# First weight transfer of a windowed-attention and mixture-of-experts kernel cut in two, with the middle steps of its hand-written schedule in a new order

## The chip, the core and the metric

The kernel runs on one core of one Trainium2 chip. The metric is device time in microseconds (us): the median of several runs, each of them one execution of the whole program. Times inside the program come from one profiled execution and count from the first instruction.

## The reference

Eight sentences of 576 tokens go through causal sliding-window attention (8 heads of 64, a window of 64 tokens), and then each sentence as a whole through one of eight experts:

```python
scores = np.where(mask, scale * (q @ k.T), -1e9)     # mask: 0 <= pos_q - pos_k < 64
attn = exp(scores - max) / sum
x = attn @ v                                          # (8, 576, 512)
logits = x.mean(axis=1) @ w_gate                      # one expert for each sentence
e = argmax(logits); gate = softmax(logits)[e]
out[b] = gate * (np.maximum(x[b] @ w1[e], 0) @ w2[e]) # w1[e]: 512x1024, w2[e]: 1024x512
```

All inputs and the output are 32-bit floats in the chip's main memory (HBM). Nothing of a sentence's expert weights can be loaded before the sentence's attention is done, since the choice of the expert depends on it.

## The kernel before

**Units and chunks.** The attention of a sentence (a batch b) is five units: four pairs of heads over the first 512 tokens, and one tail unit with the last 64 tokens of all heads. Unit number u is 5b + i, with i = 4 for the tail. A unit passes through these steps, each named by a letter and the unit's number:

- T (L225, tail L232): TensorE turns q and k round against an identity matrix, into PSUM. U and k (L242, L246, L252, L255) copy the two halves to SBUF, on ScalarE (Ua, ka) or VectorE (Ud, kd).
- S (L275): scores, sixteen small matmuls. With b in the name (Sb) two matmuls ahead of them (L269) put the mask in as a bias; without it, step K (L297) multiplies the mask in afterwards, on VectorE.
- E (L288, L291): exponential on ScalarE. l (L309, L314): row sums on TensorE. n and R (L351, L357): logarithm and exponential on ScalarE, which make a reciprocal.
- A (L331, L339): probabilities times v, on TensorE. X (L364, L370): the scaled result on VectorE, with a running sum for the gate.

The letter m in a T, S or A step takes its PSUM tile from a pool of three tiles that the experts use too; the other T, S, A and l steps have one buffer of their own each.

When the five X of batch b are done, the gate follows: g (L380, L384, VectorE), j (L392, TensorE), G (L403 to L407, VectorE: the largest logit and its index), H (L432, ScalarE), I (L438, VectorE), and P (L413), in which GpSimd loads the expert's number into a register.

The expert's work on a sentence is 18 chunks, always taken in the same order by the step c: eight of eight matmuls against w1 (L461), one for the tail tokens (L470), eight halves of four output rows against w2 (L503), and one for the tail (L512). After a chunk, ra or rd moves its result out of PSUM on ScalarE or VectorE (L446, L448, L482, L487). O and o store results.

**Loads.** Nearly all loads are issued by GpSimd, in its program's order, and turn 32-bit floats into 16-bit ones on the way: Q2b and Q2b+1 (L110: q and k of batch b, 512 KB each as they land), L (L141, L145: v of batch b, numbers 5b to 5b+4, 128 KB each and 64 KB for the fifth), t (L133: the tail of q and k, twice 64 KB), W (L423, L426: the weights; batch b has 4b and 4b+1 for the halves of w1, 4b+2 and 4b+3 for the halves of w2, 512 KB each). GpSimd's DMAs take eight semaphores in turn, so an issue waits until the DMA issued eight before it has landed. Step V (L150, L151) copies v of a batch into a shifted layout on VectorE and needs that batch's first four L.

**Order.** Each engine runs its instructions in the order in which the string OPS names the steps. OPS has 890 steps, read one by one at the end of the kernel function. A chunk's first operand waits for its weights, and everything behind it on TensorE waits with it.

Of the kernel before, what the change touches and what calls it, by code (L numbers as in the profile page):

```python
# [1 line left out]
OPS = (  # L2
# [35 lines left out]
).split()  # L38

# [17 lines left out]
def kernel(  # L57
# [13 lines left out]
    F = moe_w1.shape[2]  # L71
# [51 lines left out]
    def cast_raw(x, lohi, e):  # L123
        lo, hi = int(lohi) // 10, int(lohi) % 10
        tiles, tag = ((qms, "qm"), (kms, "km"))[x]
        if 0 not in tiles:
            tiles[0] = ld.tile([128, H, 256], BF16, tag=tag, name=tag)
        copy(e)(out=tiles[0][:, lo:hi], in_=raw[x, lo])
# [29 lines left out]
    mb = const.tile([128, 4, 16], FP16)  # L158
# [76 lines left out]
    def copy(e):  # L235
        return nc.scalar.copy if e == 'a' else nc.vector.tensor_copy
# [176 lines left out]
        nc.gpsimd.load(ereg, eidxs[b][0:1, 0:1])  # L413
        esl[b] = nc.gpsimd.snap(ereg, donate=True)

    def load_w(x):
        b, c = divmod(x, 4)
        s = WSLOT[b]
        e = ds(esl[b], 1)
        kw = {}  # L420
        if c < 2:
            cols = ts(c, F // 2)
            nc.gpsimd.dma_start(out=w1b[s][:, :, cols], in_=w1e[e].squeeze(0)[:, :, cols], **kw)  # L423
        else:
            fbs = ts(c - 2, 4)
            nc.gpsimd.dma_start(out=w2b[s][:, fbs], in_=w2e[e].squeeze(0)[:, fbs], **kw)  # L426
# [63 lines left out]
    def store(eng):  # L490
        for n, (dst, src) in enumerate(outq.pop(0)):
            (nc.scalar if n and eng is nc.sync else eng).dma_start(out=dst, in_=src)  # L492
# [43 lines left out]
    with tc.manual_schedule():  # L536
        for op in OPS:
            c, x = op[0], op[1:].lstrip("abdm")
            e = op[1:len(op) - len(x)]
            if c == "c":  # L540
                todo.pop(0)()
            elif c in "oO":
                store(nc.sync if c == "o" else nc.gpsimd)
            elif c == "r":
                evac.pop(0)(e)
            elif c == "F":
                wps = ps_m.tile([128, 512], FP32, tag="mo", name="wps")
                for _ in range(int(x)):
                    nc.tensor.matmul(out=wps, lhsT=warm[:, 0:128], rhs=warm, start=True, stop=True)
            elif c in setup_ops:  # L550
                setup_ops[c]()
            elif c == "Y":
                load_raw(int(x.split(".")[0]), x.partition(".")[2])
            elif c == "C":
                cast_raw(int(x.split(".")[0]), x.partition(".")[2], e)
            elif c == "Q":
                load_qk(int(x.split(".")[0]), x.partition(".")[2])
            elif c in batch_ops:
                batch_ops[c](int(x))
            elif c in unit_eops:  # L560
                unit_eops[c](*units[int(x)], e)
            else:
                unit_ops[c](*units[int(x)])
# [30 lines left out]
```

## Time and profile before

| | before |
|---|---|
| median of 3 runs | 203.64 us (203.49 to 203.77) |
| profiled execution, first to last instruction | 201.9 us |
| profiled execution's own whole time | not told by its page |
| TensorE (matmul) busy | 183.5 us, 91% |
| ScalarE busy | 131.8 us, 65% |
| VectorE busy | 119.9 us, 59% |
| GpSimd busy (issuing DMAs) | 111.0 us, 55% |
| moved by DMA, as it lands | 41.16 MB, mean 204 GB/s |

The profiled span is 1.7 us shorter than the median, which includes what lies around the program's instructions. In the profile PE is TensorE, PEld its weight loads, DVE VectorE, ACT ScalarE, POOL GpSimd. A timeline row gives start and length in us, engine, line, operation, out<-in, shapes and a count, and in brackets the idle time before it with what ended that. A matmul's row ends with a modelled end, so the time that a group really takes is the distance to the next group's start. A DMA's row on POOL is its issue; when it landed is told by the list of DMA issues, as us from the issue's start.

### The profile page before, as it was taken

Reading aid. Unit: us, or ns where it says so; the run is one execution under the profiler, and the core shown is the slowest. Engines: PE = TensorE matmul, PEld = TensorE weight load, DVE = VectorE, ACT = ScalarE, POOL = GpSimd, SP = SyncE. Lnnn points to the kernel's source line nnn. Section 1 sums busy time; section 2 is a strip of 40 time slices with the busy share of each in tenths; the row PEclk is TensorE's granted clock in tenths of the full one; section 3 lists DMA queues with packets and bytes.
Section 4 is the critical chain, followed back from the end, with each engine's and each line's share of the span. In section 5 each row is a group of like instructions: output and inputs, shape, how many; then the busy total and the mean of one; then the engine's idle time right before and its main releaser. Section 6 shows DMA issues by size and latency. Waiting matters only on the chain.

```text
span 201.9 us, 8105 instructions
## 1 busy us (share of the span) xinstructions
PE 183.5 (91%) x3518; PEld 124.2 (62%) x3522; DVE 119.9 (59%) x347; ACT 131.8 (65%) x247; POOL 111.0 (55%) x158
## 2 busy tenths in 40 slices
PE   0487886899999999999999999999999999999991
PEld 0455564656677756577667666676656666776760
DVE  3527989595477546895877457966494651216410
ACT  2179998876599578977779975757787436321121
POOL 7985939235931593478633552439452716553561
PEclk9999999999999999999999999999999999999998
DMA  6999999999999999999999999999999999999693
GB/s 135 175 188 159 194 162 198 199 198 174 196 201 197 170 198 193 174 201 167 200 206 200 169 195 223 259 208 137 183 237 243 266 254 212 274 212 301 235 325 134
DMA packets 83346, 41.16 MB, mean 204 GB/s; under 512 B 48080, under 2 KB 80976, under 8 KB 83312
## 3 DMA queue, kind: packets, MB, share of 16 engines
q0 software_dynamic: 81936, 39.72, 138.5%
q1 hardware_dynamic: 768, 0.85, 1.3%
q8 instruction: 27, 0.44, 0.8%
q10 hardware_dynamic: 608, 0.08, 0.2%
q14 instruction: 7, 0.06, 0.1%
HBM read 61.88 MB, written 9.44 MB: 353 GB/s over the span
## 4 chain that ended last, share of the span: by engine, by line
PE 77%; DMA 9%; POOL 7%; issue 3%; DVE 2%; ACT 1%; POOLq 0%; DVEq 0%; ACTq 0%
PE ph L461 28%; PE po L503 25%; DMA vw<-in_v_dram 9%; PE tp L225 5%; PE ph L470 4%; PE s L275 4%; PE av L331 3%; PE po L512 3%; PE lb L309 3%; POOL vw L141 2%; POOL km L110 2%; POOL qm L110 1%; POOL out_dram L492 1%; PE gps L392 1%; POOL qkt L133 1%
## 5 line engine op out<-in xcount | busy, mean ns | idle before, releaser
L503 PE MATMUL po<-w2b,hm 128*64 128x512 f16 x512 | 60.1, 379 | 0.0
L461 PE MATMUL ph<-xm,w1b 128*64 128x512 f16 x512 | 60.0, 379 | 0.0
L461 PEld LDWEIGHTS <-w1b 128*64 128x64 f16 x512 | 31.7, 110 | 18.7 <-issue 0.4
L503 PEld LDWEIGHTS <-hm 128*64 128x64 f16 x512 | 30.1, 110 | 19.3
L141 POOL DMA_DIRECT2D vw<-in_v_dram x32 | 28.9, 910 | 13.3 <-DMA w1b<-in_moe_w_dram 4.3
L446 ACT ACTIVATE hm<-ph,gw 128x512 f16<-128x512 f32 x39 | 26.6, 693 | 13.4 <-PE ph L461 13.3
L492 POOL DMA_DIRECT2D out_dram<-ob x31 | 17.2, 557 | 25.0 <-DMA w1b<-in_moe_w_dram 7.0
L351 ACT ACTIVATE ln<-lb 128x512 f32<-128x512 f32 (+1 forms) x40 | 22.5, 563 | 11.8 <-PE lb L309 8.6
L364 DVE CUSTOM_DVE_ANT_0 xm<-av,rl 128x512 f16<-128x512 f32 x32 | 21.6, 686 | 10.4 <-PE av L331 9.5
L482 ACT COPY ob<-po 128x512 f32<-128x512 f32 x18 | 10.6, 586 | 23.6 <-PE po L503 23.6
L448 DVE TENSOR_SCALAR hm<-ph,gw 128x512 f16<-128x512 f32 x25 | 18.7, 748 | 12.1 <-PE ph L461 11.6
L357 ACT ACTIVATE rl<-ln 128x512 f32<-128x512 f32 (+1 forms) x40 | 23.3, 594 | 1.5 <-DVE pool L364 1.3
L225 PE MATMUL tp<-ident,qm 128*64 128x128 bf16 x256 | 13.8, 232 | 7.4 <-DMA qm<-in_q_dram 6.9
L288 ACT ACTIVATE pe<-s 128x1024 f16<-128x1024 f32 x19 | 19.5, 1028 | 1.4 <-PE s L275 0.7
L297 DVE TENSOR_TENSOR pe<-pe,mask 128x1024 f16<-128x1024 f16 x24 | 16.3, 687 | 3.9 <-ACT pe L288 3.1
L252 ACT COPY kT<-tp 128x512 bf16<-128x512 bf16 x19 | 11.2, 597 | 9.0 <-PE tp L225 8.0
L225 PEld LDWEIGHTS <-qm 128*64 128x64 bf16 x256 | 10.7, 118 | 10.0 <-DMA qm<-in_q_dram 6.9
L482 DVE COPY ob<-po 128x512 f32<-128x512 f32 x14 | 9.7, 690 | 10.7 <-PE po L503 10.5
L423 POOL DMA_DIRECT2D w1b<-in_moe_w_dram x16 | 12.6, 785 | 5.9 <-DMA vw<-in_v_dram 2.9
L275 PEld LDWEIGHTS <-kT 64*128 64x128 bf16 x576 | 10.1, 95 | 8.9 <-issue 5.6
L331 PEld LDWEIGHTS <-vw 128*64 128x64 f16 x512 | 12.4, 112 | 4.7 <-issue 1.2
L225 PE MATMUL tp<-ident,km 128*64 128x128 bf16 x256 | 13.9, 231 | 1.4 <-DMA km<-in_k_dram 0.9
(80 smaller groups left out, 267.2 us busy)
## 6 DMA issues: line engine op xcount, KB each, us to landing
w1b<-in_moe_w_dram POOLq DMA_DIRECT2D x16, 512.0 KB, 9.3
w2b<-in_moe_w_dram POOLq DMA_DIRECT2D x16, 512.0 KB, 13.4
out_dram<-ob POOLq DMA_DIRECT2D x31, 256.0 KB, 8.1
vw<-in_v_dram POOLq DMA_DIRECT2D x32, 128.0 KB, 9.0
km<-in_k_dram POOLq DMA_DIRECT2D x7, 512.0 KB, 9.3
qm<-in_q_dram POOLq DMA_DIRECT2D x7, 512.0 KB, 9.0
out_dram<-obt POOLq DMA_DIRECT2D x14, 64.0 KB, 7.7
qkt<-in_q_dram POOLq DMA_DIRECT2D x8, 64.0 KB, 7.6
```

The costliest lines, as they stand in the source:

```text
L141: nc.gpsimd.dma_start(out=vt[:, 2 * J + 1], in_=v[b, :, 128 * J:128 * J + 128].rearrange("h c d -> c h d"))
L225: nc.tensor.transpose(tp[p0:p0 + 64, n, r], t[:, 2 * i + hh, ts(r, 64)], ident)
L288: nc.scalar.activation(out=po, in_=sp[0], func=AF.Exp, scale=scale)
L351: nc.scalar.activation(out=ln, in_=lb[:, 0:n], func=AF.Ln)
L357: nc.scalar.activation(out=rl, in_=lns.pop((b, i)), func=AF.Exp, scale=-1.0)
L364: nc.vector.tensor_tensor_reduce(out=xm[:, i], in0=av.rearrange("q r p -> q (r p)"), in1=rl, scale=1.0, scalar=0.0, op0=ALU.mult, op1=ALU.add,
L446: nc.scalar.activation(out=o, in_=i, func=AF.Relu, scale=g)
L448: nc.vector.tensor_scalar(out=o, in0=i, scalar1=g, scalar2=0.0, op0=ALU.mult, op1=ALU.max)
L461: nc.tensor.matmul(out=ph[64 * c:64 * c + 64], lhsT=w1t[:, kb, ts(2 * ft + c, 64)], rhs=xm[:, kb], start=(kb == 0), stop=(kb == 3), skip_g ...
L482: copy(e)(out=ob, in_=po)
L492: (nc.scalar if n and eng is nc.sync else eng).dma_start(out=dst, in_=src)
L503: nc.tensor.matmul(out=po[64 * c:64 * c + 64], lhsT=hm[:, fb, ts(2 * r + c, 64)], rhs=w2t[:, fb], start=(fb == 0), stop=(fb == 7), skip_gr ...
```

## The change

Two things change. The step W0 (the first half of the first batch's w1) becomes two transfers, W0.0 and W0.1, of a quarter of w1 each: 256 of the 1024 columns, enough for two w1 chunks each. And the steps from the 75th to about the 560th stand in a new order. Among them some copies change between ScalarE and VectorE, ten ra become rd, and some S change between b and no b (four Sb before, three after, one of these for a tail unit). The steps before and behind keep their order, so that the whole list has 892 steps.

```diff
-    "n2 R1 R4 l0 V0 A3 Ud6 L7 Am1 n0 E5 T9 X3 Am2 Ud9 S7 R2 L8 E7 Ud8 X1 R0 l5 X2 L6 n5 Smb6 "
...
-    "A9 W2 E10 S13 kd18 Ud18 L13 Tm15 Ud15 l10 Am8 R8 W3 kd15 ka17 T16 K14 L11 c X8 L14 n10 "
...
+    "E12 n8 K12 W0.1 Am7 E14 R6 A6 l12 Sm10 S11 n12 E10 T17 X7 l9 X6 A9 c ka17 n9 W1 Ud17 c R9 "
+    "K10 l10 E11 X9 rd R8 c rd S13 A8 X8 E13 rd T16 c rd W2 L11 g1 c c rd W3 Ua16 n10 ra j1 "
...
-    def load_w(x):
+    def load_w(x, part=""):
...
-            cols = ts(c, F // 2)
+            cols = ts(2 * c + int(part), F // 4) if part else ts(c, F // 2)
...
+            elif c == "W":
+                load_w(int(x.split(".")[0]), x.partition(".")[2])
```

OPS is one line shorter, so line numbers behind it are one lower than before up to load_w. Three places follow at which the order differs; a row has line, operation, out<-in with the buffers' numbers, and the written shape.

GpSimd up to the first weights, before (qkt is the tail of q and k, qm and km are q and k of batch 3, w1b0 the first batch's w1, vw2 v of batch 2, TENSOR_LOAD the step P0):

```order
L141 DMA vw1_92<-in_v_dram 128x8x64 x4
L133 DMA qkt_647<-in_q_dram 64x8x64
L133 DMA qkt_647<-in_k_dram 64x8x64
L110 DMA qm_703<-in_q_dram 128x8x256
L110 DMA km_820<-in_k_dram 128x8x256
L413 TENSOR_LOAD eidx_733
L423 ISA
L423 DMA w1b0_96<-in_moe_w1_dram 128x4x512
L141 DMA vw2_93<-in_v_dram 128x8x64
L423 ISA
L423 DMA w1b0_96<-in_moe_w1_dram 128x4x512
```

The same place after:

```order
L132 DMA qkt_554<-in_q_dram 64x8x64
L132 DMA qkt_554<-in_k_dram 64x8x64
L140 DMA vw1_92<-in_v_dram 128x8x64 x3
L109 DMA qm_741<-in_q_dram 128x8x256
L109 DMA km_755<-in_k_dram 128x8x256
L412 TENSOR_LOAD eidx_745
L422 ISA
L422 DMA w1b0_96<-in_moe_w1_dram 128x4x256
L422 ISA
L422 DMA w1b0_96<-in_moe_w1_dram 128x4x256
L422 ISA
L422 DMA w1b0_96<-in_moe_w1_dram 128x4x512
```

One load of v stays ahead of the tail loads (not shown after) and three move behind them; the same bytes as before stand ahead of the first weights, and no load of v lies between the parts of w1 any more.

VectorE from the second shift copy of batch 1 to the third of its attention results (ISA rows that write xm are X; those that write pool alone belong to the X ahead), before:

```order
L151 COPY vw1_92<-vw1_92 64x4x512
L242 COPY qt_826<-tp_751 128x512
L438 RECIPROCAL gw_829<-gsum_746 128x1
L252 COPY kT0_94<-tp_768 128x512
L364 ISA xm_841,pool_843<-av_861,rl_785 128x512
L364 ISA pool_843 128x1
L246 COPY qtt_896<-tpt_832 128x256
L255 COPY kT0_94<-tpt_832 128x4x64
L364 ISA xm_841,pool_843<-av_844,rl_791 128x512
L364 ISA pool_843 128x1
L364 ISA xm_841,pool_843<-av_879,rl_905 128x512
```

The same place after:

```order
L150 COPY vw1_92<-vw1_92 64x4x512
L245 COPY qtt_801<-tpt_704 128x256
L437 RECIPROCAL gw_803<-gsum_753 128x1
L254 COPY kT0_94<-tpt_704 128x4x64
L241 COPY qt_808<-tp_679 128x512
L241 COPY qt_833<-tp_784 128x512
L363 ISA xm_835,pool_837<-av_838,rl_739 128x512
L363 ISA pool_837 128x1
L296 TENSOR_TENSOR pe_873<-pe_873,mask_111 128x1024
L363 ISA xm_835,pool_837<-av_879,rl_828 128x512
L363 ISA pool_837 128x1
L363 ISA xm_835,pool_837<-av_901,rl_899 128x512
```

A copy of k has gone to ScalarE, a copy of q (Ud11) has come behind the shift, and a mask product (K12) that did not exist stands between the results.

GpSimd up to the first weights of batch 2 (w1b2), before:

```order
L141 DMA vw0_91<-in_v_dram 128x8x64 x3
L145 DMA vw0_91<-in_v_dram 64x8x64
L413 TENSOR_LOAD eidx_1688
L133 DMA qkt_1703<-in_q_dram 64x8x64
L133 DMA qkt_1703<-in_k_dram 64x8x64
L110 DMA qm_1710<-in_q_dram 128x8x256
L423 ISA
L423 DMA w1b2_98<-in_moe_w1_dram 128x4x512
```

The same place after:

```order
L109 DMA km_2046<-in_k_dram 128x8x256
L132 DMA qkt_2057<-in_q_dram 64x8x64
L132 DMA qkt_2057<-in_k_dram 64x8x64
L140 DMA vw1_92<-in_v_dram 128x8x64 x2
L412 TENSOR_LOAD eidx_1700
L109 DMA qm_2123<-in_q_dram 128x8x256
L144 DMA vw0_91<-in_v_dram 64x8x64
L422 ISA
L422 DMA w1b2_98<-in_moe_w1_dram 128x4x512
```

A 512 KB load of k (Q11, km_2046) and two loads of v for batch 4, which stood behind these weights before, now stand ahead of them.

65 rows, old and new, of the table OPS are left out of this document.

## Prediction

> **What bounds the kernel now.** I read the page first, then the engines by stage, then the chain that ended last around the first chunk. The page has the span and the busy shares in 40 slices:
>
> ```profile
> span 201.9 us, 8105 instructions
> PE 183.5 (91%) x3518; PEld 124.2 (62%) x3522; DVE 119.9 (59%) x347; ACT 131.8 (65%) x247; POOL 111.0 (55%) x158
> PE   0487886899999999999999999999999999999991
> DMA  6999999999999999999999999999999999999693
> ```
>
> Two resources are full: TensorE from the eighth slice (40 us) on, the DMA engines from the second. The table by stage (PE, PEld, DVE, ACT, POOL busy, then clock, DMA share, GB/s) says it in numbers:
>
> ```profile
> 8.00:40.00 32.00, 25.37 (x642) 18.42 (x648) 21.04 (x62) 27.58 (x52) 22.03 (x27) 1.00 1.76 182
> 41.00:120.00 79.00, 79.00 (x1576) 52.18 (x1572) 53.83 (x158) 62.05 (x118) 42.46 (x53) 1.00 1.62 190
> ```
>
> From 41 to 120 us PE is busy 79.00 of 79.00 us. What can be won lies ahead of 41 us, where PE stands idle 6.6 of 32 us. The work is fixed, so the end comes earlier only if the first chunk, from which on PE never runs dry, starts earlier by more than the work that is left for later. The chain shows what leads to that chunk:
>
> ```profile
> 22.68 8.52 DMA vw<-in_v_dram
> 31.32 0.88 DVE vw L150
> 32.22 0.76 DVE vw L151
> ...
> 38.18 0.50 issue
> ...
> 41.01 4.32 PE ph L461 x40
> ```
>
> It runs from a load of v that lands at 31.2 us over V1 (31.32 to 32.98) through attention steps to PE, where forty matmuls, five chunks, then take 4.32: 0.86 a chunk. The loads come in a row, the next landing as soon as the one ahead is through. The issues on POOL and, below them, each one's time to landing (the first row is the second tail load, then k of batch 3, W0, and the load of v behind W0):
>
> ```profile
> 24.45 0.69 POOL L133 DMA_DIRECT2D qkt<-in_k_dram  x1 [0.20 <-issue]
> 27.82 0.88 POOL L110 DMA_DIRECT2D km<-in_k_dram  x1 [1.72 <-DVE grd L384]
> 30.04 0.75 POOL L423 DMA_DIRECT2D w1b<-in_moe_w_dram  x1 [1.34 <-DVE kT L252]
> 30.78 0.89 POOL L141 DMA_DIRECT2D vw<-in_v_dram  x1
> ...
> qkt<-in_k_dram POOLq DMA_DIRECT2D x1, 64.0 KB, 7.2
> km<-in_k_dram POOLq DMA_DIRECT2D x1, 512.0 KB, 9.0
> w1b<-in_moe_w_dram POOLq DMA_DIRECT2D x1, 512.0 KB, 9.4
> vw<-in_v_dram POOLq DMA_DIRECT2D x1, 128.0 KB, 9.5
> ```
>
> So k lands at 36.8, W0 at 39.4, v at 40.3: 512 KB take 2.6 us of the queue, 128 KB 0.87, 64 KB half of that, 0.43. W0 is issued nine us before it lands; the queue ahead decides, not the issue. On PE, this stands just before the first chunk (a T has two rows, the second left out):
>
> ```profile
> 39.12 0.41 PE L275 MATMUL s<-qt,kT 64*128 64x64 bf16 x16
> 39.45 0.41 PE L225 MATMUL tp<-ident,qm 128*64 128x128 bf16 x8
> ...
> 39.93 0.38 PE L309 MATMUL lb<-pe,ones 128*64 128x512 f16 x2
> 40.14 0.42 PE L331 MATMUL av<-pe,vw 128*64 128x64 f16 x16
> 40.39 0.39 PE L225 MATMUL tp<-ident,qm 128*64 128x128 bf16 x8
> ...
> 40.84 0.38 PE L461 MATMUL ph<-xm,w1b 128*64 128x512 f16 x2
> ```
>
> From start to start a score step costs 0.33 us, a T 0.45, a row sum 0.22, an A 0.25. The first chunk starts at 40.84.
>
> **The change, part by part.**
>
> *W0 in two.* Ahead of W0.0 stand the same loads as ahead of W0, so it lands half a transfer earlier: 36.8 + 1.3 = 38.1 us; W0.1 lands at 39.4, where W0 did; W1, with no v ahead, at 42.0. The added transfer costs POOL one more issue, 0.75 us, under a queue that is nine us deep. Its rows are half as long, 512 bytes as they land, as those of q and k are, and 512 KB of k took 2.6 us as W0 did: I take nothing for that, and 0.1 us as the upper end. That W0.0 comes later because the gate is later: T14 now stands ahead of j0 on PE and needs the tail loads; behind it wait j0, G0, P0 and all weights. The set of v and tail loads that landed last at 24.45 + 7.2 = 31.6 is the same, and three loads of v now come behind the tails: these land at 31.6 - 3 x 0.87 = 29.0. The gate then passes at about 29.3 on PE, where these rows had it at 28.02, with VectorE's index search behind it, and the weights' issue after that:
>
> ```profile
> 28.02 0.29 PE L392 MATMUL gps<-grd,ones 128*64 128x8 f32 x4 [0.30 <-ACT ln L351]
> 28.36 0.17 DVE L403 MAX8 gmx<-gps 128x8 f32<-128x8 f32 x1 [0.60 <-PE gps L392]
> ```
>
> So the issue slips by 1.3 us, to 31.3, and the queue still has 5.5 us of work when it comes: no cost. Cover gone (an issue after some 33 us), each us would cost one.
>
> [...]
>
> *When PE is ready for the first chunk.* VectorE must get from V1 to X6, which frees the buffer of A9, the last step ahead of the chunk. The groups' means:
>
> ```profile
> L364 DVE CUSTOM_DVE_ANT_0 xm<-av,rl 128x512 f16<-128x512 f32 x32 | 21.6, 686 | 10.4 <-PE av L331 9.5 <-PE al L339 0.5 <-ACT rl L357 0.2
> L297 DVE TENSOR_TENSOR pe<-pe,mask 128x1024 f16<-128x1024 f16 x24 | 16.3, 687 | 3.9 <-ACT pe L288 3.1 <-ACT pe L291 0.5
> L242 DVE COPY qt<-tp 128x512 bf16<-128x512 bf16 x25 | 10.4, 417 | 8.0 <-PE tp L225 3.6 <-ACT kT L252 3.2 <-PE s L275 1.2
> ```
>
> V1 starts when the last v lands, 31.6 + 0.1, and takes 1.66: 33.4. Then come three small ones (0.29 at most each, as the row of one below shows: 0.9 at most), Ud11 and Ud13 (0.83), X5, X7, X6 (2.06) and K12 (0.69): at most 4.5 in all, X6 done at 37.7 to 37.9, A9 from there 0.15: PE ready at 37.9 to 38.05.
>
> ScalarE's side is l9, which waits for n12. n7 stood at 27.34; with Ua6 more ahead of it (0.6), a smaller copy less (0.3) and later row sums I put it at 28.2. From n7 to n12 ScalarE has two exponentials of 1024, one in two halves of 256, and thirteen others of about 0.58.
>
> ```profile
> 34.61 0.29 DVE L246 COPY qtt<-tpt 128x256 bf16<-128x256 bf16 x1
> ...
> L288 ACT ACTIVATE pe<-s 128x1024 f16<-128x1024 f32 x19 | 19.5, 1028 | 1.4 <-PE s L275 0.7 <-PE av L331 0.5
> ...
> 27.34 0.63 ACT L351 ACTIVATE ln<-lb 128x512 f32<-128x512 f32 x1
> ...
> 30.78 1.08 ACT L252 COPY kT<-tp 128x512 bf16<-128x512 bf16 x2
> 31.72 0.63 ACT L351 ACTIVATE ln<-lb 128x512 f32<-128x512 f32 x1
> ```
>
> By such lengths that is 2 x 1.03 + 0.76 + 13 x 0.58 = 10.4, or 38.6 at the end of n12. But ScalarE's rows overlap: from the start of the two copies to the next start it is 0.94, not 1.08, and each ends 0.1 behind the next one's start; sixteen times 0.1 make 37.0. With l9 and A9 behind it, 0.3, PE is ready between 37.3 and 38.9 by ScalarE. I take VectorE's 37.9, since overlap is what the rows show. The later of ready and landed: **first chunk at 38.15**, up to 38.9.
>
> *What is left for later.* T18, S13, Tm15, l10, Am8 and T16 stood ahead of the first chunk and now stand behind it: 3 x 0.45 + 0.33 + 0.22 + 0.25 = 2.15 us of PE that must still run when PE is full. The mask matmuls that fall away were all ahead of the first chunk, where PE waits anyway: nothing.
>
> *The sum.* 40.84 - 38.15 = 2.69 earlier, 2.15 more to do: **0.54 us** off the profiled span, 201.9 to 201.4. The same off the median of the runs, which lies 1.7 us above the span: 203.64 to 203.1.
>
> *What must hold behind it.* Ten results move from ScalarE to VectorE and five copies the other way; VectorE gets some 5 us more in a stretch where it was busy 53.83 of 79: hidden, as long as a chunk's result leaves PSUM before the third chunk after it wants the tile. The closest place is the start:
>
> ```profile
> L448 DVE TENSOR_SCALAR hm<-ph,gw 128x512 f16<-128x512 f32 x25 | 18.7, 748 | 12.1 <-PE ph L461 11.6
> ```
>
> From X6 at 37.8 VectorE has Ud17 (0.42), K10 (0.69), X9 (taken at 1.0), three results (2.24) and X8 (0.69): the third chunk's tile is free at 42.8. PE wants it for the sixth at 38.15 + 5 x 0.86 + 1.25 (l10, S13, A8, T16) = 43.7. Cover gone, each such wait costs its length. Loads are tighter. Between W0 and W8 the queue now has twelve of 512 KB, ten of 128 and six of 64: 12 x 2.6 + 10 x 0.87 + 6 x 0.43 = 42.5, so W8 lands at 81.9. Made for the order before (11, 8, 6) this gives 77.6, and these rows say 78.15 (69.95 + 8.2), so I add 0.5: 82.4.
>
> ```profile
> 69.95 0.76 POOL L423 DMA_DIRECT2D w1b<-in_moe_w_dram  x1 [2.49 <-DMA vw<-in_v_dram]
> w1b<-in_moe_w_dram POOLq DMA_DIRECT2D x1, 512.0 KB, 8.2
> ...
> 81.45 0.82 PE L461 MATMUL ph<-xm,w1b 128*64 128x512 f16 x6
> ```
>
> PE wanted W8 at 81.45. After the change it starts 2.69 earlier but has six T, three row sums, two S and an A more before it, 2.7 + 0.66 + 0.66 + 0.25 = 4.3: 83.05. The margin shrinks from 3.3 to 0.65 us. The same count gives W7 a margin of about 0.9.
>
> **The rivals.** 0.2% of 203.64, 0.41 us, is about what a measurement of this kernel can tell from no change.
>
> *The queue falls behind (slower).* One mechanism: batch 2's weights stand behind Q11 and two more v, W8 lands after the chunk asks, and PE, full until then, stops. It decides from 0.65 us of lateness over 42 us of loads. For it: that is 1.5%, and my count was 0.5 off on the order before. Against: PE waited for no load between 41 and 120 us. Two us late would lose 1.35, less 0.54 won: +0.8, 204.4. Chance 0.17.
>
> *Every transfer has a fixed price in the queue (slower).* A lone 64 KB store issued by SyncE took 2.4 us to land, so up to 2 us may not scale with bytes:
>
> ```profile
> out_dram<-obt SPq DMA_DIRECT2D x1, 64.0 KB, 2.4
> ```
>
> If the added transfer paid 2 us in the queue, W8 would land at 84.4, 1.35 late: 204.4. Against it stand the 0.43 us of the queue's 64 KB; chance 0.03. [...]
>
> *PE isn't ready (no change).* If ScalarE takes its full lengths, the first chunk starts at 38.9 and the gain is gone (38.15 + 0.54 = 38.7 is the point); ready only at 39.4, the cut does nothing, as the whole of W0 was there by then, and 0.7 is lost. Around 203.6; chance 0.30, which takes in small waits of 0.2 to 0.5 at single chunks. A further 0.05 is for the later end, 204.3.
>
> *Waits in the rest go too (faster by more).* The row of issue, 0.50 at 38.18, may fall where PE waits anyway: 1.1 in all, 202.5. Chance 0.10.
>
> **The numbers.** Likeliest is the sum, 203.1, with 0.35 (its own range 202.8 to 203.3). Faster by over 0.2%: 0.35 + 0.10 = 0.45. Within: 0.30. Slower: 0.17 + 0.03 + 0.05 = 0.25. The range reaches from the fourth rival to the first, 202.5 to 204.4.
>
> **What would show it.** In the profile after: the first L461 matmul at 38.1 to 38.3, right behind a w1b of 256 KB; j0 at 29.3; W8's chunk at 83; PE 9 in every slice from there. Wrong if PE waits for w1b or w2b in the stage from 41 to 120, if the first chunk starts after 38.9, or if PE waits for ScalarE or VectorE among the first chunks.

## The result and the profile after

| | before | after |
|---|---|---|
| median | 203.56 us (203.23 to 203.77, 4 runs) | 206.71 us (206.62 to 206.81, 4 runs) |
| profiled execution, first to last instruction | 201.9 us | 205.1 us |
| first chunk on TensorE starts | 40.84 | 37.83 |
| from there to the last matmul | 156.50 | 162.69 |

The change makes the kernel slower: ratio 1.0149, 95% interval 1.0133 to 1.0166. The forecast was 203.1. The first chunk came 3.0 us earlier, and what stands behind it took 6.2 us longer.

The page of the kernel after, with the span, the busy shares in 40 slices, and one row of the DMA queues, which matters below (packets, MB, share of 16 engines):

```profile
span 205.1 us, 8092 instructions
PE 185.6 (91%) x3516; PEld 123.4 (60%) x3520; DVE 124.1 (60%) x353; ACT 128.4 (63%) x235; POOL 111.8 (55%) x159
PE   0588777899999798999999999999999999999991
...
q8 instruction: 27, 0.44, 0.8%
```

TensorE has two slices below 9 in its full stretch, a 7 and an 8 near 70 and 77 us. The table by stage, same columns as before:

```profile
8.00:40.00 32.00, 26.17 (x610) 18.08 (x616) 20.55 (x69) 28.32 (x54) 22.73 (x29) 1.00 1.75 184
41.00:120.00 79.00, 77.13 (x1564) 50.07 (x1558) 56.93 (x153) 55.04 (x99) 41.15 (x51) 1.00 1.58 182
```

PE now stands idle for 1.87 of 79 us where it was idle for none. The chain that ended last shows that the head of the program went as forecast (start, length, what):

```profile
21.22 7.41 DMA qkt<-in_k_dram
...
29.50 0.24 DVE eidx L403 x2
...
30.97 6.82 DMA w1b<-in_moe_w_dram
37.79 0.04 issue
37.83 1.92 PE ph L460 x16
```

W0.0 is issued at 30.97 and lands at 37.79, and the first chunk starts right behind it. PE's waits from 36 to 131 us, the whole list:

```profile
PE tp L224 <- issue: 1.3, 1, 1.3
PE s L274 <- issue: 0.6, 1, 0.6
PE ph L460 <- DMA w1b<-in_moe_w_dram: 0.5, 1, 0.5
```

The third is the wait for W0.0. The first two end with "issue": no other engine and no load that the profile shows was waited for. PE's timeline at these two places:

```profile
69.62 0.33 PE L224 MATMUL tp<-ident,qm 128*64 128x128 bf16 x5
71.24 0.27 PE L224 MATMUL tp<-ident,qm 128*64 128x128 bf16 x3 [1.29 <-issue]
...
77.21 0.20 PE L274 MATMUL s<-qt,kT 64*128 64x64 bf16 x1
77.98 0.39 PE L274 MATMUL s<-qt,kT 64*128 64x64 bf16 x15 [0.57 <-issue]
```

Both gaps lie inside a group of equal matmuls: T21 stops after five of the eight that turn q, S21 after one of sixteen. No data was waited for. What was missing, as the experiments below bear out, was the program: the instructions come by DMA as well, on queue q8. Its 27 packets hold 0.44 MB, 16 KB each, for PE's 7036 matmuls and weight loads (3516 and 3520): some 260 for each packet. Counted in order of start, all of PE's records from 0, the gaps lie at numbers 2492 and 2748, 256 apart, and every gap of this kind in every kernel below lies at 188 plus a multiple of 256 (four further on in the last of the kernels with extra work, whose trace has four more records ahead of them). The DMA queues from 68.95 to 70.00 us have:

```profile
q8 instruction: 1, 0.02, 5.7%
```

That is one packet of 5.7% of 16 engines for 1.05 us, 0.96 us; by the trace it runs from 68.99 to 69.95. PE had used up its block at 69.73, and its next matmul starts at 71.24. So this block could be used some 2.25 us after its fetch had begun (2.2 to 2.7 at all such gaps), and the fetch began 3.4 us after the block before had ended (65.56). The two make 5.7 us; PE was through the 256 instructions between in 4.17 and waited for the rest, 1.5 us. In S21 it waited 0.75.

Why here: the block that ends inside T21 ran for 4.17 us. PE's rows of it, three left out:

```profile
65.62 1.03 PE L460 MATMUL ph<-xm,w1b 128*64 128x512 f16 x8
66.58 0.29 PE L274 MATMUL s<-qtt,kT 64*128 64x64 bf16 x8
66.81 1.05 PE L460 MATMUL ph<-xm,w1b 128*64 128x512 f16 x8
...
68.36 1.18 PE L469 MATMUL ph<-xt,w1b 128*64 128x64 f16 x64
69.36 0.42 PE L330 MATMUL av<-pe,vw 128*64 128x64 f16 x16
69.62 0.33 PE L224 MATMUL tp<-ident,qm 128*64 128x128 bf16 x5
```

Two chunks of eight long matmuls stand among short ones, 64 of them in the tail chunk alone: one us for 128 instructions. In the order before, the same tail chunk comes behind 46 long matmuls in a row, and the block that ends here ran for 6.4 us:

```profile
63.49 5.17 PE L461 MATMUL ph<-xm,w1b 128*64 128x512 f16 x46
68.59 0.41 PE L275 MATMUL s<-qt,kT 64*128 64x64 bf16 x16
68.93 0.41 PE L309 MATMUL lb<-pe,ones 128*64 128x512 f16 x2
69.17 1.18 PE L470 MATMUL ph<-xt,w1b 128*64 128x64 f16 x64
```

To compare kernels I added up the starts of all matmuls behind the first chunk: what lies at block ends above the usual distance ("stalls"), what else lies above it ("other waits"), and the rest, the matmuls themselves with the usual distances between kinds ("work"):

| us | before | after | difference |
|---|---|---|---|
| work | 156.08 | 159.54 | +3.46 |
| stalls at block ends | 0.16 | 2.52 | +2.36 |
| other waits | 0.27 | 0.63 | +0.36 |
| first chunk's start | 40.84 | 37.83 | -3.01 |

The sum is +3.17, the span's difference of 3.2. Without the stalls the kernel after would still be 0.8 us behind.

### The profile page after: what moved, and what is told of

The parts are those of the page before. It is cut to its first block, busy times and chain, and to the rows that moved or that the text cites. A ratio compares the mean times of both kernels' runs of the same rounds, so it can differ in the third digit from the quotient of the medians.

```text
span 205.1 us, 8092 instructions
## 1 busy us (share of the span) xinstructions
PE 185.6 (91%) x3516; PEld 123.4 (60%) x3520; DVE 124.1 (60%) x353; ACT 128.4 (63%) x235; POOL 111.8 (55%) x159
## 4 chain that ended last, share of the span: by engine, by line
PE 67%; DMA 16%; POOL 8%; issue 6%; POOLq 1%; DVE 1%
PE ph L460 24%; PE po L502 20%; DMA w2b<-in_moe_w_dram 5%; PE tp L224 4%; DMA vw<-in_v_dram 4%; PE s L274 4%; DMA qkt<-in_k_dram 4%; PE ph L469 3%; DMA w1b<-in_moe_w_dram 3%; PE av L330 3%; PE lb L308 3%; POOL out_dram L491 3%; PE po L511 3%; POOL km L109 2%; POOL qm L109 1%
## 5 line engine op out<-in xcount | busy, mean ns | idle before, releaser
L460 PEld LDWEIGHTS <-w1b 128*64 128x64 f16 x512 | 30.5, 110 | 19.8 <-DMA w1b<-in_moe_w_dram 0.7
L447 DVE TENSOR_SCALAR hm<-ph,gw 128x512 f16<-128x512 f32 x34 | 25.0, 746 | 7.8 <-PE ph L460 7.4
L445 ACT ACTIVATE hm<-ph,gw 128x512 f16<-128x512 f32 x30 | 20.3, 690 | 13.5 <-PE ph L460 13.5
L287 ACT ACTIVATE pe<-s 128x1024 f16<-128x1024 f32 x24 | 24.7, 1027 | 5.2 <-PE s L274 3.2
L296 DVE TENSOR_TENSOR pe<-pe,mask 128x1024 f16<-128x1024 f16 x26 | 17.6, 684 | 3.3 <-ACT pe L287 2.6
L251 ACT COPY kT<-tp 128x512 bf16<-128x512 bf16 x21 | 12.5, 594 | 8.7 <-PE tp L224 7.7
L274 PEld LDWEIGHTS <-kT 64*128 64x128 bf16 x576 | 10.8, 95 | 11.3 <-issue 8.1
L422 POOL DMA_DIRECT2D w1b<-in_moe_w_dram x17 | 13.2, 779 | 7.7 <-DMA w2b<-in_moe_w_dram 3.1
L425 POOL DMA_DIRECT2D w2b<-in_moe_w_dram x16 | 12.3, 776 | 7.9 <-DMA w2b<-in_moe_w_dram 2.0
```

The source lines that it names most:

```text
L287: nc.scalar.activation(out=po, in_=sp[0], func=AF.Exp, scale=scale)
L445: nc.scalar.activation(out=o, in_=i, func=AF.Relu, scale=g)
L447: nc.vector.tensor_scalar(out=o, in0=i, scalar1=g, scalar2=0.0, op0=ALU.mult, op1=ALU.max)
L460: nc.tensor.matmul(out=ph[64 * c:64 * c + 64], lhsT=w1t[:, kb, ts(2 * ft + c, 64)], rhs=xm[:, kb], start=(kb == 0), stop=(kb == 3), skip_g ...
```

## The experiments

My theory was that the stalls come from where the block ends fall among the steps, and the rest from the work that was moved behind the first chunk. The rival was that the stalls belong to the steps (buffers, loads, semaphores), or that the second transfer costs something. The two kernels with extra work were run once each, for their profiles alone. The kernels of one group ran on one chip, beside the kernel before, whose medians there were 203.82 (first four), 203.97 (next four), 203.91 (next three) and 203.77 (the last).

**Other block ends, same order.** F issues small matmuls on data that nobody needs, at the program's head; each is two instructions.

```diff
-    Y0.24 Q0.48 Q1.48 ...
+    F72 Y0.24 Q0.48 Q1.48 ...
...
-                    nc.tensor.matmul(out=wps, lhsT=warm[:, 0:128], rhs=warm, start=True, stop=True)
+                    nc.tensor.matmul(out=wps[0:64, 0:16], lhsT=warm[:, 0:64], rhs=warm[:, 0:16],
+                                     start=True, stop=True)
```

> The changed kernel, step for step, with 72 small matmuls on zeros ahead of all other TensorE work (144 instructions, in the first 6 us, where TensorE waits for q; their result is used by nothing). Theory A (TensorE stalls where a block of 256 of its instructions ends and the next, fetched in 16 KB, isn't there yet): the block ends fall 144 instructions earlier in the program, so the gaps inside the transposes of T21 and the scores of S21 (1.48 and 0.75 us over their own time) go, and what stalls are left stand at other places, each again at a block end, the worst ahead of or inside chunk 2.h8 (about 1 us); together 1.0 to 1.5 us faster than the changed kernel, 205.2 to 205.7. Theory B (VectorE or PSUM tiles or loads are late at these places): the order is the same, the gaps stay where they are, 206.7, or later by what the 72 matmuls delay.

Measured: 207.6 us (206.44 to 208.86), ratio 1.018 (1.0136 to 1.0224). The gaps in T21 and S21 are gone and two others have come, in T22 and in a w2 chunk. The place in T22:

```profile
72.74 0.28 PE L224 MATMUL tp<-ident,qm 128*64 128x128 bf16 x3
74.40 0.33 PE L224 MATMUL tp<-ident,qm 128*64 128x128 bf16 x5 [1.39 <-issue]
```

Both lie 144 instructions earlier in the program than a block end of the kernel after, as 72 matmuls shift them. The stalls make 2.26 us against 2.52: that the two gaps go and that others come at block ends was foreseen. Their places were not (I had named chunk 2.h8, which runs through), and the gain of 1.0 to 1.5 us was not there, since the new block ends fall into dense stretches too.

The same with F128, one whole block:

> As the run with 72 matmuls, but 128 of them, 256 instructions, one whole block: the block ends stand where they stood in the program. Theory A: the gaps inside T21 and S21 come back, 206.7 within 0.3, unless the 128 take longer than TensorE's wait for q, by which the start of the head would slip by at most 1 us. If instead the extra work at the start itself helps (a TensorE that is busy earlier), this run is as fast as the one with 72. Theory B: 206.7 too, but then so is the one with 72.

Measured: 207.24 us (206.37 to 208.3), ratio 1.0171 (1.0131 to 1.0212). The gaps are back at the very matmuls, T21 after five of eight (1.45 us) and S21 after one of sixteen (0.74), 2.19 us in all. The place in T21:

```profile
71.38 0.27 PE L224 MATMUL tp<-ident,qm 128*64 128x128 bf16 x3 [1.26 <-issue]
```

Whatever the steps wait for did not change between these two kernels; the place in the block did.

The same edit with F44 in the kernel before, with its own order:

> The kernel before, step for step, with 44 small matmuls on zeros ahead (88 instructions): it moves the block ends from places with long instructions ahead of them to places with many short ones. Theory A: by the time of the 105 to 130 instructions ahead of each block end the stalls after the first chunk grow from about 0.1 to 1.3 to 2.7 us, while the 0.7 us inside T18 at 38 us goes; 204.3 to 205.8, and every new gap stands at a block end. Theory B: nothing changes, 203.6.

Measured: 206.78 us (205.97 to 207.42), ratio 1.0135 (1.0096 to 1.0175): nearly the whole loss of the change, with neither its order nor its cut, and more than the 204.3 to 205.8 expected. Its waits on PE from 41 to 131 us:

```profile
PE ph L459 <- issue: 1.2, 1, 1.2
PE ph L468 <- issue: 0.7, 1, 0.7
PE s L273 <- issue: 0.6, 1, 0.6
```

The stalls add up to 3.26 us against 0.16, and the median rose by 2.96. So block ends alone can cost this much, and the order before is fast in part because its block ends happen to fall well.

**The cut alone.** Both transfers in the order before, in W0's place:

```diff
-    Ud13 W0 I0 kd11
+    Ud13 W0.0 W0.1 I0 kd11
```

> The order before, with W0 alone cut into two transfers, one directly behind the other. If the split itself costs (a fixed price per transfer), all loads behind it land up to 2 us later and the first chunk with them: 203.6 to 205. If it costs nothing, W0's first half lands at 38.1, the chunk still waits for the order of TensorE: 203.6 within 0.3. TensorE's instructions are the same ones, so theory A expects the same stalls as before.

Measured: 203.83 us (203.18 to 205.03), ratio 1.0003 (0.9977 to 1.0028). The second transfer costs nothing that this can tell, and 2 us lie far outside the interval. In the kernel after, the two halves land 1.33 us apart, half of what 512 KB take, as the prediction had it. The 2 us of the prediction's second rival do not show in this full queue.

**Denser chunks spread out.** In the kernel after, the tail chunk and one w2 chunk of batch 1, with their copies out of PSUM, move behind two w1 chunks of batch 2, so that the blocks there hold more long matmuls:

```diff
+    todo[26:44] = [todo[n] for n in (27, 28, 29, 30, 31, 32, 33, 34, 36, 37, 38, 26, 39, 40, 41, 42, 43, 35)]
```

> The changed kernel with two of batch 1's chunks put later: 1.h8 (its 64 short matmuls, 128 instructions in 1.2 us) and 1.o4, which needs it, stand between batch 2's first chunks, where a block of 256 instructions takes TensorE 8.8 us, instead of in the block that ends inside T21 and takes 4.2 us. All work is done; the number of loads, copies and matmuls is the same. Theory A (a block end is passed no sooner than some 5.7 us behind the one before): the gap of 1.5 us inside T21 shrinks to 0.3, that of 0.75 in S21 goes or shrinks, 1.1 to 2.0 us faster than the changed kernel, 204.7 to 205.6. Theory B (late copies, PSUM tiles or loads in that stretch): no gain, 206.7, or more, since two chunks now hold PSUM tiles among batch 2's.

Measured: 207.92 us (207.61 to 208.67), ratio 1.0202 (1.0185 to 1.022), a miss. The stalls fell to 0.92, one place, and T21 and S21 run through. But other waits rose from 0.63 to 2.42, most of them short ones behind ScalarE and VectorE, and the first chunk came 0.7 us later, at 38.55. PE's waits from 38 to 131 us, all but two:

```profile
PE s L274 <- issue: 0.8, 1, 0.8
PE ph L462 <- DMA w1b<-in_moe_w_dram: 0.6, 1, 0.6
...
PE ph L471 <- DVE hm L448: 0.2, 1, 0.2
PE ph L462 <- DVE kT L251: 0.2, 1, 0.2
...
```

The 1.6 us that the stalls no longer cost went into other waits. That these come because the results are now wanted earlier is argued, not shown.

**Does the load on the DMA engines matter?** The kernel after without the steps W8 to W31, so that batches 2 to 7 use the weights of the first two batches and their results are other ones:

```diff
-    WSLOT = (0, 1, 2, 0, 1, 2, 0, 1)
+    WSLOT = (0, 1, 0, 1, 0, 1, 0, 1)
```

> The changed kernel without the weight loads of batches 2 to 7, 24 of 512 KB, which compute with the weights of batches 0 and 1 instead (their results are other ones). TensorE's instructions are the same to the last one. If the fetch of a block comes late because it stands behind bulk loads in the DMA engines, then from some 67 us on fetches follow the block end before them by under 2.5 us instead of 3.3 to 4.3, the gaps in T21 and S21 shrink from 1.48 and 0.75 to under 0.5 together, and the time is 204.2 to 205. If the pace is TensorE's own, fetches and gaps stay as they are: 206.7, less at most 0.3 for the small waits. Theory B with late loads: the gaps go, but without a change in when fetches start.

Measured: 208.84 us (208.38 to 209.28), ratio 1.0246 (1.0228 to 1.0263), a miss. The other loads moved forward and kept the DMA engines busy to 84 us, so the gaps in T21 and S21 stayed (1.38 and 0.74). Two stretches:

```profile
70.00:80.00 10.00, 8.24 (x174) 5.33 (x169) 6.71 (x16) 7.14 (x13) 4.68 (x6) 1.00 1.93 175
85.00:87.00 2.00, 2.00 (x52) 1.44 (x54) 0.32 (x2) 2.00 (x5) 0.00 (x0) 1.00 0.05 9
```

In the first, with 175 GB/s, the fetch begins 4.3 us after the first instruction of the block that is running (75.77 against 71.50); in the second, with 9 GB/s, 0.65 us after it (85.64 against 84.99). Three more fetches ahead of which the engines were idle (at 93.98, 112.14 and 131.92) begin at most 0.3 us after it; one at 122.65, in a burst of loads of over 200 GB/s, begins 5.1 us after it and makes a third stall, of 0.9 us. It points to the load, without settling it. So I measured the pace by itself, in kernels that do extra work: 48 steps of sixteen short matmuls in a row, no data waited for, in the kernel before.

```diff
+        for _ in range(48):
+            for m in range(8):
+                for hh in range(2):
+                    p0 = 64 * hh
+                    nc.tensor.matmul(out=p2[hh][:, ts(m, 64)], lhsT=warm[p0:p0 + 64, 0:128],
+                                     rhs=warm[p0:p0 + 64, 0:64], start=True, stop=True,
+                                     skip_group_check=True)
```

Placed near the program's end, where I took the DMA engines to be nearly idle, and behind two other stretches: twelve times three steps of eight long matmuls and three of sixteen short ones, then 36 times one and one.

> The kernel before with three stretches of work on zeros ahead of batch 7's chunks (used by nothing; the time as a whole says nothing): 36 times 8 matmuls of 512 columns and 36 times 16 of 64 columns, like chunks and score steps, first three and three in turn (24 changes of kind), then one and one (72 changes), then 48 score steps alone. If an interposed step costs what I took for it (0.33 us from start to start), both mixed stretches take 36 x (0.86 + 0.25 to 0.33) = 40 to 43 us. If each change of kind costs about 0.1 more than the mean inside a step, as the two traces say (0.31 from a chunk's last matmul to a score's first, 0.12 back, where inside it is 0.10 and 0.015), the second takes 24 x 0.31 = 7.4 us more. The 48 steps alone are six blocks of 256 instructions at 2.0 to 2.6 us each by their own speed: if blocks pass no faster than some 2.3 us behind a fetch, they show what the pace is with the DMA engines nearly idle: 2.3 to 3 us a block, or 5.7 if the pace is TensorE's own.

The short steps, and from the other two stretches one turn each:

```profile
185.06 0.87 PE L548 MATMUL psml<-warm 64*128 64x64 bf16 x48
...
188.57 0.87 PE L548 MATMUL psml<-warm 64*128 64x64 bf16 x48
...
224.54 1.05 PE L541 MATMUL pbig<-warm 128*64 128x512 bf16 x8
...
225.87 1.05 PE L541 MATMUL pbig<-warm 128*64 128x512 bf16 x8
...
279.60 2.04 PE L548 MATMUL psml<-warm 64*128 64x64 bf16 x128 [1.96 <-issue]
283.33 2.04 PE L548 MATMUL psml<-warm 64*128 64x64 bf16 x128 [1.69 <-issue]
```

A block of 128 short matmuls and their weight loads takes 3.73 us from start to start, though the matmuls need 2.04. In groups of three, 72 steps take 42.2 us (twelve turns of 3.51); in turn, 47.6 (36 of 1.32): 5.4 us more for 48 more changes of kind, 0.11 each. I had put it at 7.4.

The same 48 steps ahead of the first w1 chunk of batch 1, where the loads run:

> The kernel before with the 48 score-like steps alone (six blocks of 256 TensorE instructions, on zeros, used by nothing) ahead of chunk 1.h0, at some 57 us, where the DMA engines work on a queue that is some nine us deep, instead of in the tail, where the pace was 3.73 us a block. The time as a whole says nothing. If the pace comes from the fetch's wait in busy DMA engines: 5 to 6.7 us a block for the first two or three, and 3.7 once the loads have run into full buffers and the engines are idle. If the pace is TensorE's own, 3.73 us for all.

PE's timeline, and three of its stretches in the table by stage:

```profile
64.27 3.34 PE L540 MATMUL psml<-warm 64*128 64x64 bf16 x128 [2.37 <-issue]
70.47 2.82 PE L540 MATMUL psml<-warm 64*128 64x64 bf16 x128 [2.85 <-issue]
...
77.65 2.04 PE L540 MATMUL psml<-warm 64*128 64x64 bf16 x128 [1.28 <-issue]
81.11 2.04 PE L540 MATMUL psml<-warm 64*128 64x64 bf16 x128 [1.41 <-issue]
```

```profile
64.27:70.40 6.13, 3.34 (x128) 3.18 (x128) 0.00 (x0) 0.00 (x0) 0.00 (x0) 0.72 1.86 175
70.47:73.90 3.43, 2.81 (x128) 2.65 (x128) 0.00 (x0) 0.00 (x0) 0.00 (x0) 0.64 0.22 18
77.65:81.10 3.45, 2.04 (x128) 1.92 (x128) 0.00 (x0) 0.00 (x0) 0.00 (x0) 1.00 0.02 5
```

With 175 GB/s of loads a block takes 6.2 us, with 5 GB/s 3.5. Only one block ran wholly beside the loads, which were through at 70 us. That the granted clock was lower in it, 0.72, is not the reason: the next block, at 0.64 and 18 GB/s, took 3.45. The same instructions took 6.2 us a block beside the loads, 3.45 to 3.73 behind them, and 3.73 to 4.0 in the probe near the program's end; that the traffic of the DMA engines sets this pace is my reading, with one block for it.

**What the cut is worth in the new order.** The kernel after with W0 in one transfer:

```diff
-    P0 W0.0 X5 l8 Smb14 E12 n8 K12 W0.1 Am7
+    P0 W0 X5 l8 Smb14 E12 n8 K12 Am7
```

> The changed order with W0 in one transfer, at the place of the first half. The first chunk then waits for the whole of W0, 39.1 instead of 37.8: 1.3 us later. By the sum (the earlier first chunk is worth what it comes earlier) 206.7 + 1.3 = 208.0; if TensorE's pace by blocks hides it (the fetch of the block behind is what is waited for), between 207.2 and 208.0. If the cut itself costs, it is no slower than 206.7.

Measured: 208.75 us (208.13 to 210.11), ratio 1.0224 (1.0205 to 1.0243). W0 lands at 40.13, later than the 39.1 expected (its issue came 0.7 us later than in the kernel after, behind tail loads that were 0.7 later), and PE has waited 1.5 us for it. By the ratios, 1.0224 against 1.0149 with the cut on another chip, the cut is worth some 1.5 us in the new order, 0.8 to 2.2 by their intervals. The stage behind that wait, from 42 to 44 us:

```profile
42.00:44.00 2.00, 2.00 (x12) 0.83 (x10) 0.82 (x2) 0.00 (x0) 0.63 (x1) 0.50 1.51 193
```

The granted clock is 0.50 there, and PE gets through twelve matmuls.

**Which part of the order costs.** Three kernels take the order of after up to a chunk, then the missing steps of before, then the order of before to the end. Cut behind the seventh, the eighteenth, and the eleventh chunk:

```diff
     ... g1 c c rd W3 Ua16 n10 ra j1 Tm18 c
-    kd18 S17 ka16 T15 c t3 G1 Ud18 K13 K11 ra L13 H1 ...
+    L12 kd18 Ud18 L13 Tm15 Ud15 kd15 L14 R10 K11 S17 G1 H1 L10 l14 K13 c ...
```

> The changed order up to chunk 0.h6, its first chunk early and W0 cut in two, then all steps that are left in the order of the kernel before (each masked as its score step needs it). The same work as the changed kernel. From the first chunk to batch 5 TensorE changes its kind of work 8 times more than in the kernel before, where the changed kernel does it 15 times more, and behind 0.h7 its instructions stand against the blocks of 256 as they did before. Theory A: the first chunk at 37.8, no gaps of 1.5 and 0.75 us, TensorE's time behind the first chunk 156.5 + 0.4 + 8 x 0.18 = 158.3 us and small stalls of 0.2, so 0.9 to 1.2 us faster than the kernel before, 202.4 to 202.7 against 203.6, and some 4 us faster than the changed kernel. If the loss of the changed kernel lay in its head (first chunk early, the cut, the work left for later), this one is at 206 to 207. If copies on ScalarE or VectorE come late behind the splice, waits show there, and the time lies between, 203 to 205.

Measured: 207.26 us (206.8 to 208.19), ratio 1.0156 (1.0128 to 1.0185). The seam itself made a wait: a row sum of the tail unit waits until ScalarE is through with the gate's exponential.

```profile
51.33 0.30 PE L313 MATMUL lb<-pp,ones 128*64 128x256 f16 x2 [2.58 <-ACT gex L431]
```

There are no stalls at block ends, but with 2.6 us of a wait that neither order has, and a first chunk at 39.84 (the granted clock was 0.67 from 36 to 41 us), it tells nothing on the question.

```diff
     ... c A12 c ra X12 c
-    A10 rd R14 n11 Ua15 L18 P1 L14 l13 ...
+    Ud15 kd15 L14 R10 P1 Q8 A10 X10 W4 Q9 n11 ...
```

> As the splice at 0.h6, but the changed order is kept up to chunk 0.o4 at 57 us; seven score and value steps then stand in a row ahead of 1.h0. Theory A: first chunk at 37.8, the same 8 further changes of kind, and a block of 256 with that row in it takes TensorE some 5 us, so a stall of 0 to 0.8 us there, and none at T21 and S21: 202.4 to 203.5. If the loss lay ahead of 57 us: 206 to 207.

Measured: 208.32 us (207.15 to 209.57), ratio 1.0203 (1.0167 to 1.024). Again no stalls and again waits behind the first chunk, some 5.3 us in all: 1.5 for a result on VectorE, 0.9 and 0.5 for X steps, and slow matmuls behind them (the eight of a chunk at 64.19 took 1.68 us from start to start, where 0.86 is usual; the mean granted clock of this execution was 0.984, against 0.997 of the kernel after). The first chunk had waited 1.2 us for its weights. Inconclusive too.

```diff
     ... L12 c c l14 rd L10 c
-    c V2 c n14 R12 I1 ra l11 c ra c c A12 c ...
+    Ud15 kd15 L14 R10 P1 n14 Q8 rd c V2 c c ra l11 A10 X10 Am12 W4 c ...
```

> The changed order up to chunk 0.o0b, then all steps left in the order of the kernel before. In the splice at 0.h6 the steps H1 and l14 stood directly behind each other, and TensorE waited 2.65 us at l14 for ScalarE's gate exponential, which waited for VectorE; here l14 stands two chunks behind H1, as in the changed order. Theory A (loss of the changed order = changes of kind and block ends, nothing in its head): the wait at l14 goes, block ends stall for less than 0.4 us, and TensorE's time behind the first chunk is 156.5 + 0.4 + 9 x 0.18 = 158.5 us and up to 1 us of small waits, against 162.7 of the changed kernel: between 1.2 us faster and 0.5 us slower than the kernel before on the same chip, by where the loads of v let the first chunk start (37.8 to 39.8 in the runs so far). If what was saved always comes back as a wait for VectorE or ScalarE, it is 206 to 207 again.

Measured: 204.06 us (203.1 to 205.64), ratio 1.0015 (0.999 to 1.004). The profiled execution is the second fastest of the twelve, 203.3, with a span of 201.7. Here the seam holds: from 38 to 131 us PE has a single wait in the list, 0.6 us for W0.0. The first chunk starts at 37.91, the stalls are 0.00, other waits 0.55, and the work behind the first chunk is 158.68. The place of T21, in the table by stage of this kernel and of the kernel after:

```profile
68.00:80.00 12.00, 12.00 (x278) 8.41 (x276) 7.69 (x16) 7.96 (x14) 7.69 (x9) 1.00 1.69 186
```

```profile
68.00:80.00 12.00, 10.14 (x260) 7.02 (x256) 8.31 (x19) 8.59 (x15) 5.35 (x8) 1.00 1.63 189
```

So the head of the change (the cut, the earlier first chunk, the six steps left for later) is neutral, and the loss lies in the order behind some 50 us and in where its block ends fall. No kernel here is measurably faster than the one before. Whether some other number of matmuls at the head would put the block ends of the new order where they cost nothing was not tried.

## Why the prediction was wrong

**W0 in two: right.** The issue came at 30.97 (31.3 forecast), W0.0 at 37.79 (38.1), W0.1 at 39.1 (39.4), W1 at 41.7 (42.0). The issue's 0.3 comes from the tail loads, which landed at 28.6 in place of 29.0; the landings' 0.3 comes from the queue ahead, since k of batch 3 landed at 36.45 in place of 36.8. The added transfer cost nothing measurable, as the kernel with the cut alone shows.

**PE ready in time: right.** PE waited 0.54 us for W0.0, so it was ready at 37.3, earlier than the 37.9 of the sum: VectorE and ScalarE had kept up; the first chunk started at 37.83 where 38.15 was forecast, 3.01 earlier than before in place of 2.69. The third rival, PE not ready, did not come about.

**The queue behind it: right in the loads, wrong in PE.** W8 landed at 82.42, against 82.4 forecast, but its chunk asked later than the 83.05 that I gave it:

```profile
85.80 1.47 PE L460 MATMUL ph<-xm,w1b 128*64 128x512 f16 x12
```

PE had started 0.3 earlier than forecast and had lost 2.2 us to stalls and 0.85 to other things since, so the load came 3.4 us ahead of the chunk, not 0.65. PE waited for no load from 41 to 131 us: neither the queue that falls behind nor the fixed price of a transfer happened. VectorE's and ScalarE's moved copies cost no wait that the list of waits shows either.

**What is left for later: too small.** I priced six steps at the distances they have in a row, 2.15 us. PE's work behind the first chunk grew by 3.46. In the kernel with the head alone it grew by 158.68 - 156.08 = 2.60, and the rest of the order adds 159.54 - 158.68 = 0.86. In the lists of steps PE goes from one kind of step to another 148 times behind the first chunk before, 157 times with the head alone and 166 times after; nine more at the probe's 0.11 would be 1.0. That the 0.86 is this finer alternation is argued, not shown by itself; the nine that the head adds would be 1.0 as well, and there only 0.45 is found above the 2.15.

**The step that failed.** It is the sentence "the end comes earlier only if the first chunk, from which on PE never runs dry, starts earlier by more than the work that is left for later". I took "79.00 of 79.00" for a property of the kernel. It was one of the order and of its block ends: PE does run dry, of instructions, as in T21, where it was through 256 of them in 4.17 us and the next could be used only 5.7 us after these had begun. In the terms of the sum, 2.69 - 2.15 = 0.54 us earlier became 3.01 - 3.46 - 2.36 - 0.36 = -3.17, that is 3.17 later: the stalls, put at nothing, came to 2.36 more than before, the work left for later to 3.46 instead of 2.15, and other waits to 0.36. A shift of the block ends moves the stalls in both orders, so their cause is shown; that of the last 0.86 of work is not. Either of the two larger terms alone turns the gain into a loss. The kernel with the head alone bears this out: its interval of 0.999 to 1.004 leaves out the 0.9973 that 203.1 would be, although it has no stalls.

**The clue that I misread.** The row "38.18 0.50 issue" of the kernel before lies inside a T, after one of eight matmuls: it is a block end, number 1212. The fourth rival said that it may fall where PE waits anyway, and so it did: in the kernel after this block ends inside the first chunk and costs nothing. But I took it for a single wait that can only go. It was the one visible case of a price that can fall due at each of the 27 block ends, and any new order draws those places anew.

## What to carry to other kernels

A gap that ends with "issue" inside a group of equal matmuls was a fetch of instructions here: count matmuls and weight loads, and see whether the gaps are 256 apart. Before reordering a TensorE program, add up the time of each such block; here, with the loads running, the one of 4.2 us ahead of the gap in T21 cost 1.5 and the one of 6.0 ahead of that in S21 cost 0.75, while one of 4.7 and one of 5.5 in the kernel before cost next to nothing, so many short matmuls (a tail chunk, transposes, scores) should not stand together without long ones among them. And a small win that was measured in such an order can be an accident of where block ends fall: the order before lost 3 us when 44 matmuls that nobody needs were put at its head.

## What the runs showed of the hardware that was not expected

- The next block is fetched late. In the stretch at 60 to 80 us of the kernel after, the fetch begins 3.4 to 4.3 us after the first instruction of the block that is running, with the engines busy, and 0.65 us after it where they were idle (the kernel with few loads, 85.64 against 84.99). What starts the fetch stays open. None is seen further ahead: in the kernel before, each block from 13.5 us on has one of the 27 fetches begun in it.
- The block's length alone does not tell a stall: one of 4.66 us in the kernel before (79.02 to 83.68) made none: its fetch began 2.1 us behind the end of the one ahead, which had run for 8.7.
- The granted clock fell in some kernels and not in others: to 0.50 in the two us that began 1.8 us after waits of 0.5 and 1.5 us (W0 in one transfer), and to 0.72 in the dense probe beside the loads. It stayed at 1.00 through the stall of 1.3 us in T21 of the kernel after, and in the dense probe near the program's end, where PE was idle for almost half of the time. What sets the limit is not shown.
- A change from long matmuls to short ones or back is not free: 0.11 us for each change in the probe, which the busy shares do not show.
